# Compact sketch of q and repeated 1/den by SBUF transfers, numerators read from PSUM, and a new order of all work

## The chip, the cores and the metric

The kernel runs on one core of one Trainium2 chip. The metric is device time in microseconds (us); the time of a kernel is the median of its runs. Five engines work side by side and meet through semaphores: TensorE (PE, matmuls; PEld is its weight load), VectorE (DVE), ScalarE (ACT), GpSimd (POOL), and SyncE (SP), which here only issues DMA transfers.

## The reference

Two stages follow each other: linear attention with a sketched polynomial feature map, and an RWKV channel mix. Batch 4, 4 heads, 1088 positions, head size 32, sketch size r = 8, model width 128, inner width 1024, all float32.

```python
def phi(x):
    a = np.einsum('rd,bhsd->bhsr', S1, x)
    b = np.einsum('rd,bhsd->bhsr', S2, x)
    return np.einsum('bhsi,bhsj->bhsij', a, b).reshape(*x.shape[:-1], r * r)
q_p, k_p = (phi(q), phi(k))
kv = np.einsum('bhsf,bhsd->bhfd', k_p, v)
z = np.sum(k_p, axis=2)
num = np.einsum('bhsf,bhfd->bhsd', q_p, kv)
den = np.einsum('bhsf,bhf->bhs', q_p, z)[..., None] + 1e-06
x = num / den            # heads side by side: (4, 1088, 128)
...
xk = mu_k * x + (1.0 - mu_k) * x_prev      # x_prev: x one position earlier
xr = mu_r * x + (1.0 - mu_r) * x_prev
k = np.maximum(xk @ w_k, 0.0)
out = sigmoid(xr @ w_r) * (k * k @ w_v)
```

## The kernel before

All work is written as a list of numbered operations. Each has an engine (for some, one of several), a function that issues its instructions, and the tiles that it uses. The string ORDER names all of them once, in the order in which they are issued; since each engine takes its instructions in order, ORDER fixes the order on every engine and on SP's transfer queue. "85.1" means operation 85 by its second way (another engine), "26*5" means five filler matmuls in front. BANKS gives each PSUM tile one of the eight banks, in the order in which they were asked for.

A batch passes through three stages. Positions are cut into 34 blocks of 32.

- stage_k: DVE transposes k in 32 x 32 blocks (kT), PE makes both sketches of k (ab), DVE transposes them back (abT) and multiplies all pairs (phk, three parts). PE sums phk with v, and with ones for z, into kv. DVE masks this into w, and SP copies w with its halves exchanged (ws).
- stage_q, in two parts of 9 and 8 blocks (EX) and two halves z: DVE transposes q (qT). PE makes the sketches (ex): for x = 0 the sketch a, each row already repeated 8 times, for x = 1 the sketch b, repeated the other way. ACT copies a out of PSUM (a_sb, 8 copies for a batch), DVE multiplies it by b (phq, 8 of them). PE makes the numerators (num, 2 steps), and ACT copies them to SBUF (4 copies). PE makes the denominators (den); DVE transposes them (dT), adds 1e-6, takes the reciprocal and transposes again (rT). PE spreads 1/den over the partitions of each head, with a selection matrix sel (pr, four PSUM banks). DVE multiplies numerators and pr into x (four x for a batch, tile xT) and wraps the last block around for the shift by one position (wrap).
- stage_m, in chunks of 12, 12 and 10 blocks (CH): uk = (1 - mu_k) x on ACT or DVE; xk on DVE; xb, x in bfloat16, on GpSimd. For each chunk: 8 up-projections on PE (up), ReLU on ACT or DVE (kr), the square on DVE or ACT (k2), 3 down-projections of 8 matmuls (rd), the gate (rg), its sigmoid on ACT (sg), the product on DVE (o), and four stores. In names such as xk1.2, 1 is the batch and 2 the chunk.

Stages of different batches overlap: the sketches of batch 1 are made while batch 0 passes through stage_q. Loads go by SP's queue, a few of the first by ACT's. The filler matmuls (stir) multiply a zero tile.

Lines of the profile: kT L296, ab L303, abT L310, phk L317, kv L326, w L336, ws L337, qT L350, ex L362, a_sb L374, phq L379, num L393 and its copy L400, den L410, dT L420, the reciprocal L424 to L426, pr L436, x L445, wrap L450 and L451, uk L465 (ACT) or L467 (DVE), xk L469, xb L476, up L490, kr L495 or L497, k2 L499 or L501, rg L516, rd L521, sg L528, o L530, stores L534, stir L544.

Of the kernel before, what the change touches and what calls it, by code (L numbers as in the profile page):

```python
# [11 lines left out]
F32 = mybir.dt.float32  # L12
# [9 lines left out]
class _Buf:  # L22


    def __init__(self, pool, tag, bufs, shape, dtype):
        self.pool, self.tag, self.bufs, self.shape, self.dtype = pool, tag, bufs, shape, dtype
        self.t = None

# [4 lines left out]
class _Plan:  # L33
# [7 lines left out]
    def op(self, eng, cost, name, fn, need=(), uses=(), mode=None, kb=None, after=0.0, alt=(), stir=None):  # L41
        need = [n for n in need if n is not None]
        after = max([after] + [n["at"] for n in need if "at" in n])
        o = {"ways": [(eng, cost, fn)] + list(alt), "name": name, "need": [n for n in need if "at" not in n],
             "uses": list(uses), "mode": mode, "kb": kb, "after": after, "n": len(self.ops), "stir": stir}
        self.ops.append(o)
        return o
# [18 lines left out]
def kernel(  # L66
# [14 lines left out]
    nc = tc.nc  # L81
# [14 lines left out]
    HT = NB // 2  # L96
    EX = [(0, NT), (NT, HT - NT)]
# [3 lines left out]
        "0 9 11 10 14 12 15 13 25 18 26*5 2 34 32 28 36 37*4 43 41 16 178 190 20 17 158 45 159 27 30 39 "  # L101
        "33 29 35 31 19 21 22 179 38 44 191 197 42 169 195 40 167 193 46 180*4 4 199 188 332 192 321 1 "
        "160 344 184 200 196 194 186 163 198 164 3 182 23 161 162 24 53 54 345*2 171 353 165 5 55 6 351 "
        "333 50*1 347 349 47 52 181 185 51 189 48 49 183 168 56 166 59 170 58 172 57 62 173 312 187 65 7 "
        "334 338 342 174 63 83 323 336 86 340 60 84 175 73 314 74 176 87 313 335 343 66 339 78 81 79 341 "
        "76 77 82 85.1 317 61 68 315 88 102 71 89 72 318 103 316 75.1 337 70.2 319 112 177 207 208 204 "
        "206 320 201 110 113 325 111 209 322 324 205 326 327 69 203 210 213 202 80.1 212 486 105 328 214 "
        "90.1 466 106 67.2 114.1 146 147 329 64.2 107 468 108 144 211 134 135 100 101 467 145 120 141 142 "
        "346 487 354 352 348 124 216 350 469 470 104.1 219 471 472 330 331 355 356 498 488 496 494 361 "
        "217 115 109 362 363 492 490 215 357 476 475 136 116 137 224.2 473 149 153 358 221.2 474 360 359 "  # L110
        "129 130 117 118 91 8 232 233 364 366 479 95 131 132 119.1 368 477 478 367 499 501 503 218.2 365 "
        "481 480 505 489 495 491 373 507 220 139 140 497 143.1 369 148.1 482 500 504 94 259 506 266 376 "
        "483 484 92 138.1 508 121 493 227 228 225 226 264 265 93 267.1 502 377 260 485 254 255 122 96 230 "
        "231 375.2 123 256 271 133 269 370.1 245 125 127 272.1 99 257 258 222 261 249 274 229 278 268 234 "
        "512 514.1 270 273 509 262 515 372.2 516 240 510 511 447 371 513 242 263.1 128 151 237 243 223 "
        "517 235 241 448 150 449 236 439 450 244 454 455 238.1 152 451 300 440 288 289 378.2 301 276 97 "
        "295 296 154 155 374 452 277 290 156 453 456 291 518 298 520 157 437 275 239.1 438 521 299 283 "
        "457 284 522 444 461 279 519 293 98 396 523 441 247 397 280 524.1 294 297 292 285 303 286 445 442 "
        "246 302 394 420 443 446 425 526.2 530.1 248 395 426 287 126 250 253 251 421 391 531 389 532.2 "
        "390 386 392 398 307 418 460 423 424 459 419 458 462 465 387 384 427 603 422 381 382 304 385 604 "  # L120
        "428 379 380.1 553 252 281 608 432 557 609 611 606 305 607 393 591 592 596 601 602 615 306 525 "
        "545 383 598 599 388 401 308 605 527.1 543 597 600 593 544 415 533 416 282 309 310 528 400 594 "
        "610 595 546 399 535 408 409 534.1 403 463 402 536 404 464 410 413 414.1 579 580 529.2 613 411 "
        "412 548 549 547.1 538 311 614 612 405 550 551 562 417 616 540 541 574 406 539.1 429 577 552 575 "
        "567 618 578 537 568 569 617 430 542 563 407 619 431 433 434 570 436 572 564 565 571 566 556 554 "
        "573 555 576 582 435 581.1 558 560 559 584 585 561 586 583 587 588 589 590"
    )
    BANKS = (
        "054372056015416746272436032403465462631307721250511136240634316143716530157052706521532432014274"
        "263007616560411752054524720471305026165757704246716507671601271147100120305274343510263470306126"  # L130
        "73473657504533632672152467274272461077351"
    )
    KP = 1
# [13 lines left out]
    def ps(shape=(P, 512)):  # L147

        pair = shape[1:] == [KP, 512] and KP == 2
        t = _Buf(psum, None, 1, list(shape), F32)  # L150
        t.kind = "pair" if pair else "bank"
        banks.append(t)
        return t

    def dve(n, rate=0.96e3):
        return n / rate + 0.067

    def act(n, ptr=False):
        return n / 1.2e3 + (0.195 if ptr else 0.05)
# [12 lines left out]
    kin = [const.tile([P, NB, D], F32, name=f"kin{b}") for b in range(3)]  # L172
    qin = [const.tile([P, NB, D], F32, name=f"qin{b}") for b in range(3)]
    vts = [const.tile([P, H + 1, NT, D], F32, name=f"vt{b}") for b in range(3)]
    qTs = [const.tile([P, NB, 32], F32, name=f"qT{i}") for i in range(2)]
    LKB = NB * D * P * 4 / 1024

    def load_k(b, cuts, queues=(nc.sync,)):
        src = k[b].rearrange("h (sp t) d -> (h sp) t d", sp=32)
        for lo, hi, queue in zip(cuts, cuts[1:], queues):  # L180
            queue.dma_start(kin[b % 3][:, lo:hi, :], src[:, lo:hi, :])
# [39 lines left out]
    sel = const.tile([P, H, D], F32)  # L221
    nc.gpsimd.memset(sel[:], 0.0)
    for g in range(4):
        nc.gpsimd.affine_select(out=sel[:], in_=sel[:], compare_op=ALU.not_equal, fill=1.0, base=-32 * g,
                                pattern=[[-R, H], [0, D]], channel_multiplier=1)
# [3 lines left out]
    rz = [const.tile([P, NT, H, R], F32, name=f"rz{i}") for i in range(2)]  # L229
    for i in range(2):  # L230
        nc.gpsimd.memset(rz[i][:], 0.0)
# [6 lines left out]
                         _ap(mask4[:], [mask4[:].ap[0], [0, 2], [R, H], [1, R]]))  # L238
    WS = const.tile([P, 2, R * R], F32)
# [3 lines left out]
    def ws():  # L243
        nc.vector.tensor_copy(WS[:, 0].rearrange("p (j i) -> p j i", j=R), _ap(St[:, 0, :], [sp_, [0, R], [1, R]]))
        nc.vector.tensor_copy(WS[:, 1].rearrange("p (j i) -> p j i", j=R), _ap(St[:, 1, :], [sp_, [1, R], [0, R]]))

    o_ws = op("DVE", 0.25, "ws", ws, after=3.4)


    def sync(tile_, src, after, kb):  # L250
        return op("SP", 0.55, "in", lambda: nc.sync.dma_start(tile_, src), after=after, kb=kb)

    IN = {("k", 0): {"at": 3.7}, ("v", 0): {"at": 6.0}, ("q", 0): {"at": 7.2}}
    done = {}

    def arrival(nm, b):
        if (nm, b) not in IN:
            t = ARRIVE[nm][b]
            need = done[nm, b - 3] if b > 2 else []
            if nm == "k":  # L260
                IN[nm, b] = op("SP", 0.55, f"k{b}", lambda: load_k(b, [0, NB]), need, kb=LKB, after=t)
            elif nm == "q":
                IN[nm, b] = op("SP", 0.55, f"q{b}", lambda: load_q(b), need, kb=LKB, after=t)
            else:
                IN[nm, b] = [op("SP", 0.6, f"v{b}", lambda g=g: load_v(b, g, nc.sync), need, kb=LKB / 4, after=t)
                             for g in range(4)]
        return IN[nm, b] if isinstance(IN[nm, b], list) else [IN[nm, b]]

    ARRIVE = {"k": [0, 4, 12, 30], "v": [0, 4, 12, 30], "q": [0, 4, 12, 30]}
    i_mu = [sync(mu[:, 0:1], moe_mu_k.rearrange("d -> d ()"), 4.0, 1),  # L270
            sync(mu[:, 1:2], moe_mu_r.rearrange("d -> d ()"), 4.0, 1),
            sync(wr_f[:], moe_w_r, 4.0, 64)]
    i_wk = sync(wk_f[:], moe_w_k, 4.0, 512)
    i_wv = sync(wv_f[:], moe_w_v.rearrange("(c p) d -> p c d", p=P), 4.0, 512)
# [6 lines left out]
    o_mu = op("POOL", 1.9, "mu", prep, i_mu)  # L281
    o_wk = op("POOL", 1.1, "wk", lambda: nc.gpsimd.tensor_copy(wk[:], wk_f[:]), [i_wk])
    o_wv = op("POOL", 1.1, "wv", lambda: nc.gpsimd.tensor_copy(wv[:], wv_f[:]), [i_wv])

    QT = {B: []}
    XR = [None] * B

    def stage_k(b):
        kT = sb("kT", [P, NB, 32])
# [6 lines left out]
        tr = [op("DVE", dve(544) + 0.02, f"kT{b}", lambda lo=lo, hi=hi: nc.vector.transpose(  # L296
# [286 lines left out]
```

## Time and profile before

| | |
|---|---|
| median of 3 runs | 97.46 us (97.28 to 97.94) |
| profiled execution, its own time | 98.09 us |
| span in the profile | 96.0 us |
| busy: PE, PEld | 85.3 us, 53.3 us |
| busy: DVE, ACT, POOL | 82.7 us, 68.0 us, 17.1 us |
| mean granted TensorE clock | 0.984 |
| DMA: moved in all | 10.53 MB |

The span is the profiler's view of one execution; times of runs include what lies around it. Busy time is the time in which an engine has an instruction in work. On PE instructions overlap and their ends are modelled, so a busy PE is not PE at its peak. In timelines and in the chain of waits the first column is the start within the span and the second the duration, both in us; "x4" is the number of instructions that a line sums up, and what stands in brackets is the idle time of the engine in front of the first, with what ended it.

### The profile page before, as it was taken

How to read it: one execution, taken by the hardware profiler on the slowest of the kernel's cores; microseconds unless marked ns; L12 is line 12 of the kernel's file. 1: busy time of each engine (PE TensorE's matmuls, PEld its weight loads, DVE VectorE, ACT ScalarE, POOL GpSimd, SP SyncE). 2: the span in 40 equal slices, each digit the busy share in tenths (PEclk: the TensorE clock that was granted, in tenths of full speed). 3: DMA queues.
4: the chain of work that ended last, by engine and by line, in shares of the span. 5: the costliest groups of instructions: out<-in, count | busy, mean ns of one | idle time of the engine just before them, and what ended most of it. 6: DMA issues, size and time to landing. Idle time of an engine off the chain costs nothing.

```text
span 96.0 us, 3286 instructions
## 1 busy us (share of the span) xinstructions
PE 85.3 (89%) x1316; PEld 53.3 (55%) x1316; DVE 82.7 (86%) x187; ACT 68.0 (71%) x172; POOL 17.1 (18%) x45
## 2 busy tenths in 40 slices
PE   5949999799999999899998999999997999999800
PEld 1313474343575457553465579567584787789700
DVE  1268979979999999999979999999999999999510
ACT  0600540552719999998998799999999799999400
POOL 6850000180000050000087520000027000000000
PEclk9999999999999999999999999999999999999985
DMA  0999999299200396006200001220230133424442
GB/s 5 253 344 266 363 262 314 58 259 295 68 10 0 85 310 230 0 21 175 71 0 7 0 7 27 62 55 0 62 82 0 27 85 83 108 53 105 89 103 48
DMA packets 11279, 10.53 MB, mean 110 GB/s; under 512 B 1920, under 2 KB 9984, under 8 KB 11264
## 3 DMA queue, kind: packets, MB, share of 16 engines
q1 hardware_dynamic: 10608, 9.38, 36.2%
q10 hardware_dynamic: 656, 0.95, 3.3%
q8 instruction: 10, 0.16, 0.7%
q14 instruction: 5, 0.04, 0.2%
HBM read 7.83 MB, written 2.23 MB: 105 GB/s over the span
## 4 chain that ended last, share of the span: by engine, by line
PE 36%; DVE 31%; DMA 13%; ACT 10%; issue 4%; SPq 1%; DVEq 0%; ACTq 0%
DMA kin<-in_k_dram 13%; PE bank L521 12%; PE bank L490 9%; DVE phk L317 8%; ACT kr L495 7%; DVE phq L379 5%; DVE k L499 4%; DVE xT L445 4%; PE bank L362 3%; PE bank L516 3%; PE bank L303 3%; DVE xk L469 2%; PE bank L410 2%; ACT a_sb L374 2%; DVE o L530 2%
## 5 line engine op out<-in xcount | busy, mean ns | idle before, releaser
L495 ACT ACTIVATE kr<-bank 128x384 bf16<-128x384 f32 (+1 forms) x89 | 35.9, 531 | 1.7 <-PE bank L490 1.3
L490 PE MATMUL bank<-xk,wk 128*128 128x384 bf16 (+1 forms) x96 | 22.9, 318 | 0.4 <-DVE w L336 0.3
L521 PE MATMUL bank<-wv,k 128*128 128x128 bf16 x288 | 20.8, 219 | 0.6 <-DVE k L499 0.6
L374 ACT COPY a_sb<-bank 128x288 f32<-128x288 f32 (+1 forms) x32 | 10.1, 397 | 14.8 <-PE bank L362 14.8
L521 PEld LDWEIGHTS <-k 128*128 128x128 bf16 x288 | 18.2, 98 | 4.2 <-DVE k L499 1.1
L499 DVE TENSOR_TENSOR k<-kr 128x768 bf16<-128x768 bf16 (+1 forms) x34 | 17.7, 552 | 0.1
L476 POOL CAST xb<-xT 128x416 bf16<-128x416 f32 (+2 forms) x12 | 8.8, 758 | 42.8 <-DVE xT L451 27.1
L362 PE MATMUL bank<-qT,WS 32*64 32x288 f32 (+1 forms) x256 | 12.6, 411 | 0.2 <-DVE w L336 0.2
L379 DVE TENSOR_TENSOR phq<-bank,a_sb 128x288 f32<-128x288 f32 (+1 forms) x32 | 12.1, 422 | 0.6 <-PE bank L362 0.5
L317 DVE TENSOR_TENSOR phk<-abT 128x768 f32<-128x768 f32 x12 | 12.3, 1033 | 0.0
L490 PEld LDWEIGHTS <-wk 128*128 128x128 bf16 x96 | 7.9, 97 | 6.8 <-issue 5.0
L501 ACT ACTIVATE k<-kr 128x768 bf16<-128x768 bf16 (+1 forms) x14 | 11.5, 844 | 0.1
L326 PEld LDWEIGHTS bank<-vt,phk 128*64 128x64 f32 x288 | 9.1, 138 | 3.5 <-DVE phk L317 1.8
L326 PE MATMUL bank<-vt,phk 128*64 128x64 f32 x288 | 10.4, 225 | 0.6 <-DVE phk L317 0.5
L544 PE MATMUL bank<-idle 128*128 128x512 bf16 x28 | 8.5, 442 | 1.8 <-DVE idle L167 1.2
L362 PEld LDWEIGHTS bank<-qT,WS 32*64 32x64 f32 x256 | 4.8, 130 | 5.0 <-issue 1.7
L530 DVE TENSOR_TENSOR o<-bank,sg 128x384 f32<-128x384 f32 x12 | 6.6, 549 | 1.1 <-PE bank L521 1.1
L296 DVE STREAM_TRANSPOSE kT<-kin 128x544 f32<-128x544 f32 x8 | 5.8, 731 | 1.8 <-DMA kin<-in_k_dram 1.7
L469 DVE SCALAR_TENSOR_TENSOR xk<-xT,mu,uk 128x384 bf16<-128x384 f32 (+1 forms) x12 | 6.9, 578 | 0.0
L445 DVE TENSOR_TENSOR xT<-num,bank 128x256 f32<-128x256 f32 (+1 forms) x16 | 6.2, 426 | 0.5 <-PE bank L436 0.5
L544 PEld LDWEIGHTS <-idle 128*128 128x128 bf16 x28 | 2.6, 109 | 7.1 <-issue 3.2
L465 ACT ACTIVATE uk<-xT,omu 128x384 f32<-128x384 f32 (+1 forms) x8 | 4.7, 596 | 2.7 <-DVE xT L445 2.7
(56 smaller groups left out, 94.9 us busy)
## 6 DMA issues: line engine op xcount, KB each, us to landing
out_dram<-o SPq DMA_DIRECT2D x42, 48.0 KB, 1.6
vt<-in_v_dram SPq DMA_DIRECT2D x12, 144.0 KB, 5.3
qin<-in_q_dram SPq DMA_DIRECT2D x3, 544.0 KB, 6.5
kin<-in_k_dram SPq DMA_DIRECT2D x3, 544.0 KB, 6.8
qin<-in_q_dram ACTq DMA_DIRECT2D x1, 544.0 KB, 6.0
wk_f<-in_moe_w_k_dram SPq DMA_DIRECT2D x1, 512.0 KB, 6.9
wv_f<-in_moe_w_v_dram SPq DMA_DIRECT2D x1, 512.0 KB, 4.8
vt<-in_v_dram SPq DMA_DIRECT2D x4, 112.0 KB, 6.2
```

What stands on the lines that cost most here:

```text
L317: nc.vector.tensor_mul(phk[:, lo:hi].rearrange("p t h j i -> p (t h) j i"), a_bc, b_bc)
L326: nc.tensor.matmul(kv[64 * u:64 * u + 64, p, :], phk[:, t, h, :, :].rearrange("p j i -> p (j i)"), _ap(vt[:, h, t, :], [pv, [(H - h) * NT ...
L362: nc.tensor.matmul(px[x][p][z][64 * v_:64 * v_ + 64, :n * 32], WS[32 * h:32 * h + 32, x, :], fl(qT[32 * h:32 * h + 32], t, t + n), start=T ...
L374: copy(a_sb[:, :n * 32], pa[:, :n * 32])
L379: lambda p=p, t=t, pb=px[1][p][z], a_sb=a_sb, n=n: nc.vector.tensor_mul(fl(phq[:, p], t, t + n), pb[:, :n * 32], a_sb[:, :n * 32]),
L445: xo[g] = op("DVE", dve(n * 32), f"x{b}", lambda g=g, t=t, n=n, lo=lo: nc.vector.tensor_mul(fl(xT, 1 + t, 1 + t + n), fl(num, t, t + n), p ...
L490: nc.tensor.matmul(kp[:, i, :n * 32], wk[:, (c + i) * P:(c + i + 1) * P], fl(xk, c0, c0 + n), start=True, stop=True)
L495: o2.append(op("ACT", act(n * 32 * KP), f"kr{b}.{ci}", lambda kp=kp, kr=kr, i0=i0, n=n: nc.scalar.activation(kr[:, i0:i0 + KP, :n * 32], k ...
L499: ok.append(op("DVE", dve(n * 64, 1.92e3), f"k2{b}.{ci}", lambda k2=k2, kr=kr, cc=cc, n=n: nc.vector.tensor_mul(k2[:, 2 * cc:2 * cc + 2, : ...
L501: alt=[("ACT", act(n * 64) + 0.1, lambda k2=k2, kr=kr, cc=cc, n=n: nc.scalar.activation(k2[:, 2 * cc:2 * cc + 2, :n * 32], kr[:, :, :n * 3 ...
L521: nc.tensor.matmul(rd[:, i, :], k2[:, c, first[i]:first[i] + P], wv[:, c, :], start=(c == 0), stop=(c == NFF - 1))
L544: nc.tensor.matmul(t[:, :], idle[:, :P], idle[:], start=True, stop=True, skip_group_check=True)
```

## The change

The kernel's arithmetic stays; the work is cut up and placed differently.

- The sketch a of q: for batches 1 to 3 (FAR = 1) PE makes it without the repetition, 16 rows for each quarter of the positions, in 8 matmuls (ac). Two copies bring it to SBUF, and four SBUF transfers on SP's queue (as), each from 16 partitions, write it 8 times over to a_sb. Batch 0 keeps the old way.
- 1/den: the reciprocal is transposed with each value repeated for 8 columns, and four SBUF transfers on SP's queue (rs) write it four times over, to the partitions of each head (tile r). The matrix sel, the matmuls pr and the zeroed tiles rz go.
- Numerators are not copied: num is issued after den, and x reads the numerators from PSUM and 1/den from r.
- uk has GpSimd as a third way; wrap has GpSimd and ACT as ways, and the zero column of xT is written once at the start, in two fixed tiles. xb has ACT as second way. Each of the four stores of a chunk is an operation of its own and may go by SP's queue or ACT's.
- kin has two buffers instead of three, kT and uk one instead of two. In phk and in the sketches the two pair indices are exchanged.
- ORDER and BANKS are new. Read out by kind, operations whose engine or number differs (a filler matmul is counted by itself):

| | before | after |
|---|---|---|
| a copies | 32 ACT | 14 ACT |
| numerator copies | 15 ACT, 1 DVE | none |
| squares k2 | 34 DVE, 14 ACT | 26 DVE, 22 ACT |
| uk | 8 ACT, 4 DVE | 1 ACT, 11 POOL |
| xb | 12 POOL | 11 POOL, 1 ACT |
| wrap | 4 DVE | 4 POOL |
| ex (16 traced matmuls each) | 16 | 10 |
| ac, pr | none, 4 | 3, none |
| as, rs transfers | none | 12, 16 |
| stores' queue | 46 SP, 2 ACT | 42 SP, 6 ACT |
| filler matmuls | 28 | 19 |

Around the first x of batch 0 the order on DVE was "dT0 phk1 x2, rT0 qT2 phq1 x3, x0 x3, phk1 phq1 xk0.1 x0", with four phq1 ahead of it; it becomes "dT0 abT1 rT0 qT2 phk1 x2, x0 x2, phk1 xk0.1 x0 x2, kT2 x2, phq1 ...", with no phq1 ahead of it.

```diff
+    maskA = const.tile([P, 2, 2, 2, R], F32)
+    nc.gpsimd.memset(maskA[:], 0.0)
+    for z in range(2):
+        for h in range(H):
+            nc.gpsimd.memset(maskA[32 * h:32 * h + 32, z, :, h % 2 ^ z, :], 1.0)
...
+    SkA = const.tile([P, 2, 32], F32)
+    nc.vector.tensor_mul(SkA[:].rearrange("p z (w r) -> p (z w) r", r=R), _ap(St[:, 0, :], [sp_, [0, 8], [1, R]]),
+                         maskA[:].rearrange("p z w v r -> p (z w v) r"))
...
+        if b >= FAR:
+            pa = [ps() for _ in range(2)]
+            ac = sb("ac", [P, 2, NT * 32])
+
+            def compact():
+                for g in range(4):
+                    for p in range(2):
+                        nc.tensor.matmul(pa[p][32 * g:32 * g + 32, :NT * 32], SkA[64 * p:64 * p + 64, g // 2, :],
+                                         fl(qT[64 * p:64 * p + 64], TD[g], TD[g] + NT), start=True, stop=True)
...
+            def spread_a(g):
+                src = _ap(ac[32 * g:32 * g + 16], [[ac[:].ap[0][0], 16], [0, R], [1, 2 * NT * 32]])
+                nc.sync.dma_start(a_sb[:, g].rearrange("w p t -> w (p t)"), src)
...
+        def recip():
+            nc.vector.tensor_scalar(rc[:], dT[:].rearrange("p t h r -> p (t h) r")[:, :, 0], 1e-6, None, op0=ALU.add)
+            nc.vector.reciprocal(rr[:], rc[:])
+            nc.vector.transpose(rT[:].rearrange("p t (h r) -> p (t h) r", r=R), _ap(rr[:], [rr[:].ap[0], [1, NT * H], [0, R]]))
...
+        def spread_r(g):
+            lo = LO[g]
+            src = _ap(rT[32 * g:32 * g + 32, lo], [[rT[:].ap[0][0], 32], [0, 4], [1, (NT - lo) * 32]])
+            nc.sync.dma_start(fl(r, TD[g] + lo, TD[g] + NT), src)
...
-                o_num.append(op("ACT", act(n * 32), f"nc{b}", lambda keep=keep: keep(nc.scalar.copy), [on], [pn[z], num],
-                                alt=[("DVE", dve(n * 32), lambda keep=keep: keep(nc.vector.tensor_copy))]))
...
-                nc.tensor.matmul(pr[g][:, :NT * 32], sel[gs].rearrange("p h d -> p (h d)"),
-                                 rT[gs, :, :].rearrange("p t s -> p (t s)"), start=True, stop=True)
...
+                xo[g] = op("DVE", n * 32, f"x{b}", lambda pn=pn, t=t, n=n, z=z: nc.vector.tensor_mul(
+                    fl(xT, 1 + t, 1 + t + n), pn[z][:, :n * 32], fl(r, t, t + n)), [on, o_r[g]], [pn[z], r, xT])
...
+                     ("POOL", n * 32, lambda c0=c0, n=n: nc.gpsimd.tensor_scalar(
                     fl(uk, c0, c0 + n), fl(xT, c0, c0 + n), omu[:, 0:1], None, op0=ALU.mult))])
```

## The prediction

> **What bounds the kernel now.** I read the summary of busy time, then the busy time by stretches of the span, then the chain of waits, then single instructions in the timeline. The stretches say most (columns: stretch and its length, then the busy time of each engine with its instruction count, the granted TensorE clock, the DMA share and GB/s):
>
> ```profile
> 14.00:20.00 6.00, 5.09 (x102) 2.46 (x102) 5.48 (x14) 1.79 (x7) 1.16 (x3) 1.00 0.63 186
> 20.00:30.00 10.00, 9.96 (x195) 5.46 (x190) 9.80 (x23) 4.80 (x16) 1.18 (x2) 1.00 0.50 143
> ...
> 50.00:60.00 10.00, 9.46 (x186) 7.16 (x181) 9.96 (x24) 8.88 (x21) 4.23 (x5) 1.00 0.05 10
> 60.00:70.00 10.00, 9.82 (x138) 6.38 (x136) 9.86 (x25) 9.95 (x26) 0.00 (x0) 1.00 0.22 48
> ...
> 80.00:90.00 10.00, 10.00 (x142) 8.58 (x140) 9.86 (x23) 9.71 (x26) 0.00 (x0) 1.00 0.39 86
> ```
>
> The third busy column, VectorE (DVE), has hardly a gap from 20 us on; PE and ACT are nearly as full from 30 us on. But a busy PE overstates its work. Where PE runs freely in the chain, eight down-projection matmuls take 0.45 us, an up-projection 0.14 to 0.16, six gate matmuls 0.34: 36, 96 and 12 of these are 35 us. The float32 steps still to come at 30 us (6 kv of 0.8, 6 ex of 0.67, 6 num of 0.5, 3 den of 1.0, 4 ab of 0.57, 3 pr of 0.7) are 19: together 54 us of 61. So I take DVE as the bound from 20 to 91 us. The chain of waits shows how batch 0 reaches the first up-projection (start, duration, what):
>
> ```profile
> 17.59 1.04 PE bank L544 x4
> ...
> 22.20 0.48 DVE dT L420
> 22.68 1.71 DVE phk L317 x2
> ...
> 25.01 0.48 DVE rT L426
> ...
> 26.07 0.96 DVE phq L379 x3
> 27.03 0.11 issue
> 27.14 1.11 DVE xT L445 x3
> ```
>
> Work of batch 1 (phk, phq) stands on DVE ahead of and between the steps of batch 0, and four filler matmuls stand on PE. The first xk follows at 29.39, the first up-projection at 30.05 us.
>
> **Removed from DVE after the first xk.** By the two orders, DVE keeps 26 of 34 squares (k2): three took 1.49 us (384 columns) or 1.28 (320), so 8 x 0.48 = 3.8 us. The 4 uk on DVE go to GpSimd (59.28 to 59.60 us start to start): 1.3. One numerator copy: 0.3. Four wraps, 0.09 on the path each (the zeroing is done once at the start): 0.4. Together 5.8 us. Moved to behind the first xk: the 8 phq of batch 1, 0.36 each (four in 1.38 to 1.51 us), 2.9, and one more x of batch 0, 0.4. Net for this part: -2.5 us.
>
> **Ahead of the first xk.** The same 8 phq and one x leave this part: -3.3 us. Four of the phq and two phk (3.4 us) no longer stand ahead of rT of batch 0, so rT should end near 25.5 - 3.4 = 22.1 us.
>
> **1/den by transfers.** PE's four selection matmuls per batch (3.3 us in all) go; instead SP issues four transfers of 144 KB (two 128) behind rT, which x waits for. No such SBUF transfer is in the trace. The nearest rows are v loads of the same size, in the stretches 14 to 25 and 25 to 36 us, and a 32 KB SBUF transfer, ws, in the latter (KB each, median us from issue to landing):
>
> ```profile
> vt<-in_v_dram SPq DMA_DIRECT2D x2, 144.0 KB, 5.3
> ...
> vt<-in_v_dram SPq DMA_DIRECT2D x2, 144.0 KB, 2.7
> ws<-w SPq DMA_DIRECT2D x2, 32.0 KB, 1.8
> ```
>
> So 1.8 to 5.3 us; I take 2.7, as most of the loads are over by then, plus 0.5 us for an issue (four v loads took 2.01 us of SP): the first x can run 3.2 us after rT. Cover on DVE between rT and the first x, by the new order: batch 0 a qT and two phk, 0.71 + 1.84 = 2.55; batch 1 o, phk, two qT, three phq, w, 3.9; batch 2 two phk, xk, o, 2.65; batch 3 five k2, kr, two o, 3.9. Waits: 0.65 in batch 0, 0.55 in batch 2, none in 1 and 3: +1.2 us. Behind a waiting x on DVE stand the next batch's transposes and phq, so a wait there is paid in full. Behind rs on SP stand the as transfers, v loads, and stores.
>
> **The a sketch.** For batches 1 to 3 eight narrow matmuls, two copies and four SBUF transfers of 288 KB replace 16 matmuls and 8 copies per batch. ACT loses 18 copies of a and 15 of numerators (0.32 each where four stand in a row, 10.6 us) and 7 uk (0.59, 4.1), and takes 8 squares (0.82, 6.6) and one xb (0.4): 7.7 us freed. PE loses six ex steps (0.67 each, 4.0) and the 3.3, and takes three compact sketches: 16 traced matmuls each, as in an ex, 2.0 if alike. Neither sets the end by this trace, so I count nothing. The transfers: by the 144 KB row once to twice its 2.7 us, I take 4.1. The first is issued behind the four rs at 24.6 us and lands at 28.7; phq of batch 1 is due about 29.7: hidden, with 1 us to spare; batches 2 and 3 are issued far ahead.
>
> In the Trainium skill, "SBUF — State Buffer", section "Door 1: The DMA port swizzle", 16 partitions reach only 4 of 16 DMA ports, about 104 GB/s; by that I estimate 2.8 us of moving per transfer from its 16 source partitions, and twice that for two that share ports, and phq of batch 1 would wait about 2 us. No run shows it yet.
>
> **GpSimd.** It takes 11 of 12 uk and the wraps, so wrap, uk and xb of a batch then run there in a row. Its price is not in the trace. The nearest row is the same operation with a per-partition scalar, and the casts (start, duration):
>
> ```profile
> 19.01 0.61 POOL L278 TENSOR_SCALAR wr<-wr_f,mu 128x128 bf16<-128x128 f32 x1
> ...
> 33.53 1.38 POOL L476 CAST xb<-xT 128x416 bf16<-128x416 f32 x3 [12.35 <-DVE xT L451]
> ...
> 71.31 2.41 POOL L476 CAST xb<-xT 128x384 bf16<-128x384 f32 x3 [15.23 <-DVE uk L467]
> ```
>
> Low end 0.46 us each (three casts in 1.38); high end 1.45 (0.19 for omu's 2 columns, 0.61 for 128, drawn on to 384). I take 1.0, between a cast and the wr line. In the new order DVE has 1.3 to 2.3 us of other work between the last x needed and the first xk of batches 1 to 3, so this is covered; at 1.45, batch 3 would wait 0.3.
>
> It also slows DVE. The squares beside those last three casts:
>
> ```profile
> 71.28 2.85 DVE L499 TENSOR_TENSOR k<-kr 128x768 bf16<-128x768 bf16 x4
> ...
> 86.23 1.49 DVE L499 TENSOR_TENSOR k<-kr 128x768 bf16<-128x768 bf16 x3
> ```
>
> Four take 2.85 us where 2.0 would do: 0.85 lost in 2.41 us of GpSimd, 0.36 per us. Three phk beside casts lost 0.31, 0.75 and 0.25, so the old order loses about 2.1 us. The new one has 11 x 1.0 + 11 x 0.5 = 16.5 us of GpSimd; squares, phk and xk, which read two SBUF operands, are 32 of 75 us of DVE, so 16.5 x 0.43 x 0.36 = 2.6 us, with ends 1.6 and 3.2. Net +0.5 us (-0.5 to +1.1).
>
> The rule behind it, in the Trainium skill, "SBUF — State Buffer", section "Who interferes with whom", speaks against the change: a DVE instruction with two SBUF inputs and a GpSimd one that reads SBUF exclude each other, and the second blocks fully. By that all of 16.5 x 0.43 = 7.1 us would be lost; the trace agrees that they collide, but shows 0.36 of it.
>
> Nine of 28 filler matmuls go; the clock was 1.00 in every stretch to 90 us, so I count nothing. The setup on GpSimd (11 memsets, near 0.1 us each, in place of 2.1 us for sel and rz) and one more DVE product of 0.23 us lie ahead of the k load's landing, for which DVE waits 1.06 us now. The tail from the last o (91.5) to 96.0 us stays: its last stores go out by two queues before and after.
>
> **Sum.** -2.5 - 3.3 + 1.2 + 0.5 = -4.1 us: the span 96.0 becomes 91.9. The profiled execution took 98.09 us, 2.1 more than its span and 0.6 above the median 97.46; from the median, 93.4 us.
>
> **Rivals.**
> - *More gain (91.1 us).* The order puts waits nowhere and a uk costs as a cast: no 1.2, and -0.5 instead of +0.5: -6.3 us. For it: ACT, full in 30 to 40 and 60 to 70 us, is 7.7 us lighter, which could also close small gaps.
> - *GpSimd excludes DVE wholly (97.9).* 7.1 instead of 2.6 us is +4.5 on the forecast. Against it: the 0.36 measured. For it: uk is longer than a cast, so more work collides. Ends by the price of uk, 95.4 and 99.7.
> - *1/den lands late: slower.* Place: x of each batch on DVE. Batches 0 and 2 lose one for one beyond 2.7 us of landing, 1 and 3 beyond 3.4. Extra 2 x (L - 2.7) + 2 x (L - 3.4) reaches the gain of 4.1 at L = 4.1 us; at the loaded row's 5.3 it is 9.0 and the time 102.4. For it: the as transfers (288 KB each) share the queue. Against: the DMA share is 0.05 to 0.25 from 40 to 80 us.
> - *No change (97).* The early part's 3.3 us is lost again waiting for the as transfers of batch 1.
> - That the change does not do what it says has no place: the steps are written out in the order.
>
> **Numbers.** Forecast 0.55 (its own range 92 to 95.5), more gain 0.23, exclusion 0.09, late 1/den 0.09, no change 0.04. Predicted 93.4. With 2 in 10 left out (the late case, most of the exclusion, the far end of the gain) the range is 90.0 to 97.0. One per cent is 0.97 us, about what a measurement here can tell from no change: faster takes the first two and a third of the exclusion, 0.81; same 0.07 (no change, a third of the exclusion); slower 0.12.
>
> **What would show it.** Right: DVE busy near 76 us; first xk near 27 us; idle before x under 1 us per batch; k2 and phk longer by a few tenths beside GpSimd. Wrong: DVE idle before x or phq ended by the transfers; uk over 1.5 us; k2 at twice 0.5; TensorE clock under 1.00 after 14 us; PE full while DVE has gaps, which would make PE the bound and my DVE sum void.

## The result, and the profile after

The changed kernel takes 112.53 us (median of 4 runs, 112.30 to 113.24) beside 97.70 us for the kernel before on the same chip (4 runs, 97.28 to 98.01): a ratio of 1.153, with a 95% interval of 1.146 to 1.161. The prediction said 93.4 us, with a range up to 97.0: wrong in sign. The profiled execution took 112.72 us, its span is 110.9 us.

The page's first part and its DMA issues (KB each, median us from issue to landing):

```profile
PE 87.0 (78%) x1227; PEld 53.0 (48%) x1227; DVE 77.8 (70%) x167; ACT 62.4 (56%) x141; POOL 27.6 (25%) x63
...
a_sb<-ac SPq DMA_DIRECT2D x12, 288.0 KB, 6.1
vt<-in_v_dram SPq DMA_DIRECT2D x12, 144.0 KB, 5.2
...
r<-rT SPq DMA_DIRECT2D x8, 144.0 KB, 4.6
r<-rT SPq DMA_DIRECT2D x8, 128.0 KB, 3.6
```

DVE is busy for 77.8 us where it was 82.7, and ACT for 62.4 where it was 68.0: the work did leave both engines. But DVE is now idle for 33 us of its span, 13 before. The busy times by stretches say where (columns as in the prediction: PE, PEld, DVE, ACT, GpSimd, granted clock, DMA share, GB/s):

```profile
14.00:20.00 6.00, 5.83 (x86) 2.12 (x77) 6.00 (x16) 1.31 (x4) 1.38 (x3) 1.00 0.57 151
...
30.00:40.00 10.00, 6.69 (x71) 3.08 (x72) 5.39 (x14) 5.77 (x14) 1.97 (x2) 0.97 0.80 170
...
50.00:60.00 10.00, 5.98 (x92) 2.59 (x77) 5.83 (x15) 5.27 (x12) 5.23 (x7) 1.00 0.64 108
60.00:70.00 10.00, 7.71 (x105) 4.15 (x105) 6.65 (x13) 5.92 (x15) 0.00 (x0) 0.83 0.85 146
...
90.00:100.00 10.00, 10.00 (x115) 8.21 (x114) 9.72 (x21) 8.85 (x22) 5.85 (x7) 0.83 0.32 65
```

From 14 to 20 us and from 90 to 100 us DVE is full, as it was. In the three stretches shown between them DVE is idle for a third to nearly half of the time, PE and ACT are not full either, and the DMA share is 0.64 to 0.85 where it was 0.05 and 0.22 from 50 to 70 us. The DMA engines are busy but do not move much: 108 and 146 GB/s, while the kernel before reached 143 GB/s at a share of 0.50. What DVE and PE wait for (us in total, times, longest):

```profile
DVE xT L454 <- DMA r<-rT: 9.4, 4, 5.1
...
DVE phq L400 <- DMA a_sb<-ac: 7.5, 3, 3.1
...
DVE qT L344 <- DMA qin<-in_q_dram: 2.4, 1, 2.4
...
PE bank L321 <- DMA vt<-in_v_dram: 2.1, 2, 1.4
```

DVE, which the prediction took as the bound, waits 19.3 us for transfers: 9.4 for 1/den, 7.5 for the sketches a, 2.4 for a load of q that stands behind them. In the chain of waits (start, duration) the transfers are among the longest links; the only other one of this length behind 20 us is a load of k (7.09 us, from 43.54):

```profile
25.22 6.71 DMA a_sb<-ac
...
51.27 7.52 DMA a_sb<-ac
...
66.03 6.81 DMA r<-rT
...
84.42 4.52 DMA r<-rT
```

The early part went as foreseen. Batch 0 on DVE (start, duration):

```profile
20.88 0.48 DVE L426 STREAM_TRANSPOSE rT<-rr 128x288 f32<-128x288 f32 x1
...
24.87 0.79 DVE L454 TENSOR_TENSOR xT<-bank,r 128x288 f32<-128x288 f32 x2 [0.90 <-DMA r<-rT]
25.57 0.95 DVE L312 TENSOR_TENSOR phk<-abT 128x768 f32<-128x768 f32 x1
26.44 0.61 DVE L477 SCALAR_TENSOR_TENSOR xk<-xT,mu,uk 128x384 bf16<-128x384 f32 x1
```

The first xk starts at 26.44 us, 2.95 us earlier than before. What was won there, and 15 us more, is lost after it.

### The profile page after: what moved, and what is told of

Its sections match the earlier page's. It is cut to its first block, busy times and chain, and to the rows that moved or that the text cites. A ratio compares the mean times of both kernels' runs of the same rounds, so it can differ in the third digit from the quotient of the medians.

```text
span 110.9 us, 3105 instructions
## 1 busy us (share of the span) xinstructions
PE 87.0 (78%) x1227; PEld 53.0 (48%) x1227; DVE 77.8 (70%) x167; ACT 62.4 (56%) x141; POOL 27.6 (25%) x63
## 2 busy tenths in 40 slices
DMA packets 15310, 16.29 MB, mean 147 GB/s; under 512 B 2368, under 2 KB 12480, under 8 KB 15296
## 3 DMA queue, kind: packets, MB, share of 16 engines
HBM read 7.83 MB, written 2.23 MB: 91 GB/s over the span
## 4 chain that ended last, share of the span: by engine, by line
DMA 35%; DVE 23%; PE 19%; SPq 12%; POOL 5%; issue 3%; DVEq 0%; POOLq 0%
DMA a_sb<-ac 13%; DMA kin<-in_k_dram 11%; DMA r<-rT 10%; PE bank L525 6%; PE bank L496 6%; DVE phq L400 4%; SPq L371 4%; DVE phk L312 3%; POOL uk L475 3%; DVE qT L344 3%; SPq L433 2%; PE bank L520 2%; SPq L181 2%; PE bank L409 2%; SPq L332 2%
## 5 line engine op out<-in xcount | busy, mean ns | idle before, releaser
L499 ACT ACTIVATE kr<-bank 128x384 bf16<-128x384 f32 (+1 forms) x89 | 37.3, 494 | 19.3 <-PE bank L496 18.7
L475 POOL TENSOR_SCALAR uk<-xT,omu 128x384 f32<-128x384 f32 (+1 forms) x11 | 14.1, 1284 | 15.7 <-DVE xT L454 15.6
L400 DVE TENSOR_TENSOR phq<-bank,a_sb 128x256 f32<-128x256 f32 (+1 forms) x32 | 12.3, 427 | 8.0 <-DMA a_sb<-ac 7.5
L505 ACT ACTIVATE k<-kr 128x768 bf16<-128x768 bf16 (+1 forms) x22 | 17.7, 828 | 0.0
L503 DVE TENSOR_TENSOR k<-kr 128x768 bf16<-128x768 bf16 (+1 forms) x26 | 13.1, 541 | 0.0
L454 DVE TENSOR_TENSOR xT<-bank,r 128x288 f32<-128x288 f32 (+1 forms) x16 | 6.2, 433 | 9.4 <-DMA r<-rT 9.4
L382 PE MATMUL bank<-qT,WS 32*64 32x256 f32 (+1 forms) x160 | 9.3, 410 | 1.3 <-DVE qT L344 0.8
L298 PE MATMUL bank<-kT,Skb 128*32 128x288 f32 x64 | 5.7, 415 | 3.1 <-DVE phq L400 2.5
L531 ACT ACTIVATE sg<-bank 128x384 f32<-128x384 f32 x12 | 6.1, 535 | 2.2 <-PE bank L520 2.1
L344 DVE STREAM_TRANSPOSE qT<-qin 128x512 f32<-128x512 f32 (+1 forms) x8 | 5.7, 716 | 2.4 <-DMA qin<-in_q_dram 2.4
L481 POOL CAST xb<-xT 128x320 bf16<-128x320 f32 (+2 forms) x11 | 5.8, 538 | 6.0 <-DVE xT L454 6.0
```

The lines of the kernel that those rows point to most:

```text
L344: nc.vector.transpose(qT[:].rearrange("p (z t) s -> p z (t s)", z=2)[:, :, 32 * c0:32 * (c0 + n)], qin[b % 3][:].rearrange("p (z t) d -> p ...
L382: nc.tensor.matmul(px[p][z][64 * v_:64 * v_ + 64, :n * 32], WS[32 * h:32 * h + 32, x, :], fl(qT[32 * h:32 * h + 32], t, t + n), start=True ...
L400: lambda p=p, t=t, g=g, lo=lo, pb=px[1][p][z], n=n: nc.vector.tensor_mul(fl(phq[:, p], t, t + n), pb[:, :n * 32], a_sb[:, g, p, lo:lo + n ...
L475: ("POOL", n * 32, lambda c0=c0, n=n: nc.gpsimd.tensor_scalar(fl(uk, c0, c0 + n), fl(xT, c0, c0 + n), omu[:, 0:1], None, op0=ALU.mult))])
L499: o2.append(op("ACT", n * 32, f"kr{b}.{ci}", lambda kp=kp, kr=kr, i=i, n=n: nc.scalar.activation(kr[:, i, :n * 32], kp[:, :n * 32], ACTF.R ...
L503: ok.append(op("DVE", n * 64, f"k2{b}.{ci}", lambda k2=k2, kr=kr, cc=cc, n=n: nc.vector.tensor_mul(k2[:, 2 * cc:2 * cc + 2, :n * 32], kr[: ...
```

## The experiments

Theory after the result: the DMA engines are the new bound between 20 and 90 us. The twelve transfers of a read 16 partitions each, move slowly, and whatever stands behind them is late. Rivals: the transfers of 1/den are to blame; SP's line of issues is, not the engines behind it; the new order itself is bad, whatever the transfers do.

**1 to 3: each set of transfers left out, then both.** The tile that they would write is replaced by a constant one; the matmuls and copies that make their sources stay. So no_as multiplies by a constant in place of a in batches 1 to 3, no_rs by 1 in place of 1/den, no_both does both.

```diff
-                nc.sync.dma_start(a_sb[:, g].rearrange("w p t -> w (p t)"), src)    # no_as, no_both
+                pass
...
-            nc.sync.dma_start(fl(r, TD[g] + lo, TD[g] + NT), src)                   # no_rs, no_both
+            pass
```

> The 12 a transfers of batches 1 to 3 are left out; phq of these batches multiplies by a constant tile instead. Theory 1 (the SBUF transfers fill the DMA engines and SP's queue, and DVE waits for them and for the loads behind them): the a transfers are 3.5 of the 5.8 MB added and stand in front of rs, v and q loads, so without them rs lands in about 3 us, v in about 3, and the time is 95 to 99 us. Theory 2 (the new order with GpSimd in it is slow by itself, and the waits only show where it is late): less than 5 us of the 15 are won, 108 us or more.

> The 16 transfers of 1/den are left out; x multiplies by a constant tile instead. Theory 1: the 9.4 us that x waits for them go, but the a transfers still hold up phq and the loads: 102 to 106 us. Theory 2: 108 us or more.

> Both kinds of transfers are left out, with constant tiles in their place; all instructions on PE, DVE, ACT and GpSimd stay, in the same order. Theory 1: what is left is the sum of the prediction without its 1.2 us of waits, 91 to 94 us, GpSimd included. Theory 2: still over 105 us. Between the two, 95 to 105, both have a part.

One run each, beside 97.86 us for the kernel before on that chip: no_as 96.62, no_rs 102.75, no_both 91.02. All three fall inside what theory 1 gave. From 91.0, the 1/den transfers alone cost 5.6 us, those of a alone 11.7, both 21.5 (with 112.53); the other 4.2 us appear only when both are there. Without transfers the engines are full again; no_both by stretches:

```profile
30.00:40.00 10.00, 10.00 (x184) 6.25 (x177) 9.93 (x22) 9.69 (x23) 1.05 (x1) 1.00 0.54 168
...
60.00:70.00 10.00, 9.94 (x143) 7.12 (x141) 9.45 (x24) 9.83 (x25) 2.93 (x6) 1.00 0.17 34
```

So the order is not to blame: with its transfers free it is 6.8 us faster than the kernel before. But 1/den is not harmless either; no_as still waits for it, at a landing of 3.3 us (144 KB):

```profile
DVE xT L456 <- DMA r<-rT: 4.9, 6, 1.3
```

**4: the transfers alone (micro).** A kernel that computes nothing of the reference: one transfer, then four in a row, from 16, 32 or 128 partitions, each followed by a DVE copy that reads the tile written.

```diff
+        for g in range(4):
+            nc.sync.dma_start(d[g][:], _ap(t[32 * g:32 * g + 16], [[t[:].ap[0][0], 16], [0, 8], [1, N]]))
...
+            nc.sync.dma_start(d[g][:], _ap(t[32 * g:32 * g + 32], [[t[:].ap[0][0], 32], [0, 4], [1, N]]))
...
+            nc.sync.dma_start(d[g][:], _ap(t[:], [[t[:].ap[0][0], P], [1, N]]))
```

> Only transfers, each kind alone or four at once, one kind after the other; nothing of the reference is computed and the output is zeros. Theory 1a (the few source partitions are what is slow): four transfers of 288 KB from 16 partitions each take over 1.5 times the four from 128 partitions, and one alone also. Theory 1b (any SBUF transfer of this size costs that much, whatever its source): the two differ by less than 15%, and both take longer than four loads of 288 KB from HBM. For 1/den, 32 partitions against 128, the same question at 144 KB.

Issues on SP (start, duration of four issues) for 288 KB from 16, 32 and 128 partitions:

```profile
14.32 6.35 SPq L60 DMA_DIRECT2D a_four<-s  x4
27.48 4.63 SPq L64 DMA_DIRECT2D a_four<-s  x4
35.69 2.47 SPq L68 DMA_DIRECT2D a_four<-s  x4
```

and the copies on DVE that start when each has landed, the four from 16 partitions and then the last from 32 and from 128:

```profile
19.36 0.15 DVE L41 COPY s<-a_four 128x1 f32<-128x1 f32 x1 [5.06 <-DMA a_four<-s]
21.90 0.15 DVE L41 COPY s<-a_four 128x1 f32<-128x1 f32 x1 [2.39 <-DMA a_four<-s]
24.85 0.15 DVE L41 COPY s<-a_four 128x1 f32<-128x1 f32 x1 [2.80 <-DMA a_four<-s]
27.30 0.15 DVE L41 COPY s<-a_four 128x1 f32<-128x1 f32 x1 [2.29 <-DMA a_four<-s]
...
35.51 0.15 DVE L41 COPY s<-a_four 128x1 f32<-128x1 f32 x1 [1.09 <-DMA a_four<-s]
...
40.36 0.15 DVE L41 COPY s<-a_four 128x1 f32<-128x1 f32 x1 [0.59 <-DMA a_four<-s]
```

From 16 partitions, four take 13.0 us (14.32 to 27.30) and land about 2.6 us apart, one behind the other although their sources lie in four different places. From 32 they take 8.0 us and land 1.28 apart, from 128 4.7 us and 0.72 apart. By these distances the same 288 KB move at 113, 230 and 410 GB/s. The rule that the prediction cited, in the Trainium skill's "SBUF — State Buffer", section "Door 1: The DMA port swizzle", lets the rate depend on the ports that a transfer's partitions reach. The trace agrees, with the partitions of the source: the prediction's estimate by that rule, 2.8 us of moving per transfer, stands beside 2.6 measured. Four transfers as 1/den needs them (144 KB from 32 partitions) take 4.8 us, and a single one lands after 2.7 (9.17 to 11.84).

**5: the a transfers issued by ACT (as_act).** This takes them out of SP's line and leaves their bytes and their sources.

```diff
-                nc.sync.dma_start(a_sb[:, g].rearrange("w p t -> w (p t)"), src)
+                nc.scalar.dma_start(a_sb[:, g].rearrange("w p t -> w (p t)"), src)
```

> The 12 a transfers are issued by ACT instead of SP, at the same places of the order, so SP's own issues and those behind them no longer stand in line with them. If what costs the time is the line at SP, rs, v and ws are issued on time and land in 3 to 4 us: 100 to 105 us. If it is that the DMA engines themselves are taken by slow reads from 16 partitions, rs and v land as late as before, however they are issued, and ACT stands still during its own issues: 109 us or more.

Measured 114.27 us (before: 97.88): no gain, DVE still waits 9.2 us for 1/den and 7.0 for a. SP's own issues stay slow although no a transfer stands in its line any more; the four of 1/den in batch 2 took 6.20 us in the change (from 66.03) and take 8.16 us here (from 63.62). So the a transfers hold up the others without standing in their line; what both queues share is the limit, not SP's line by itself. (ACT pays for its own issues here, up to 2.86 us for one.) The Trainium skill's "DMA: Bandwidth & Descriptors", section "Issuing engines are not separate DMA queues", says that a second issuing engine brings no second set of DMA engines; this run agrees.

**6: the same bytes from 32 partitions (as32).** In the change PE already writes each row of the compact sketch twice (32 rows for each quarter of the positions), and a transfer reads 16 of them. Here the two copies are laid out as neighbours, so that a transfer reads 32 partitions and repeats four times instead of eight.

```diff
-    maskA = const.tile([P, 2, 2, 2, R], F32)
+    maskA = const.tile([P, 2, 2, R, 2], F32)
...
-                src = _ap(ac[32 * g:32 * g + 16], [[ac[:].ap[0][0], 16], [0, R], [1, 2 * NT * 32]])
+                src = _ap(ac[32 * g:32 * g + 32], [[ac[:].ap[0][0], 32], [0, 4], [1, 2 * NT * 32]])
```

> The two copies of the compact sketch that PE makes anyway are laid out as neighbours, so that each a transfer reads 32 partitions four times over instead of 16 partitions eight times; bytes, instructions and result are the same. With transfers alone on the chip, four took 8.0 us from 32 partitions and 12.9 from 16. If the span of the source is the cause, some 5 us of DMA time less per batch take away a third to a half of the 15.9 us that the a transfers cost: 104 to 108 us. If the bytes or the number of transfers were the cause, nothing changes: over 111.

Measured 105.08 us (before: 97.88). Nothing but the source of the transfers and the setup of their columns differs (15310 DMA packets and 16.29 MB in both), and 7.4 us of the 14.8 are gone. The issue row:

```profile
a_sb<-ac SPq DMA_DIRECT2D x12, 288.0 KB, 4.5
```

**7 and 8: as32 with half the bytes (as32_bf), and with two of four 1/den transfers issued by ACT (as32_bf_ract).** Both round a to bfloat16.

```diff
-        a_sb = sb("a_sb", [P, 4, 2, NT * 32])
+        a_sb = sb("a_sb", [P, 4, 2, NT * 32], BF16)
...
-            ac = sb("ac", [P, 2, NT * 32])
+            ac = sb("ac", [P, 2, NT * 32], BF16)
...
-            nc.sync.dma_start(fl(r, TD[g] + lo, TD[g] + NT), src)                               # ract only
+            (nc.scalar if g in (2, 0) else nc.sync).dma_start(fl(r, TD[g] + lo, TD[g] + NT), src)
```

> As the one before, and the compact sketch and its repeated copy are kept in bfloat16, half the bytes (the sketch a of q is rounded to bfloat16). By the times of transfers alone, some 4 to 4.5 us per batch instead of 12.9: the a transfers then cost 2 to 4 us in place of 15.9, 98 to 101 us. If a fixed cost for each transfer or its issue were what counts, it stays over 103.

> As the one before, and two of the four 1/den transfers of each batch are issued by ACT, so that the four issues of 0.6 us each stand in two lines. If x waits for the line of issues, 1 to 3 us less than the one before; if it waits for the landing itself, the same within 0.7 us; if ACT loses more by waiting for rT than x gains, more time.

as32_bf took 96.62 us, below the 98 to 101 that were expected and as much as no_as: at 144 KB from 32 partitions the a transfers cost nothing that shows. as32_bf_ract took 100.81: x waits 7.1 us in place of 4.6. The largest part is in batch 0: ACT's second issue came at 26.13 us, 5.2 us behind the end of rT, because a uk stood ahead of it on ACT and waited there for the first x; x then waited 3.55 us for what that issue brought.

**9 to 11: the a sketch made the old way.** far4 takes the compact sketch and its transfers out for all batches and keeps 1/den by transfers and uk on GpSimd. PE makes the repeated a in four steps for a batch, ACT copies it; these operations were placed into the order by hand. far4_late moves x of two batches later and issues the 1/den transfers of batch 3 in a row; far4_late_uk also puts the 11 uk of GpSimd on ACT.

```diff
-                nc.sync.dma_start(a_sb[:, g].rearrange("w p t -> w (p t)"), src)
...
+                                nc.tensor.matmul(pa[z][64 * v_:64 * v_ + 64, :n * 32], WS[32 * h:32 * h + 32, 0, :],
+                                                 fl(qT[32 * h:32 * h + 32], t, t + n), start=True, stop=True)
...
+                            copy(a_sb[:, g, p, 32 * LO[g]:32 * LO[g] + n * 32], pz[:, :n * 32])
```

> The sketch a of batches 1 to 3 is made the old way again, in four steps of two banks each (PE writes it already repeated, ACT copies 8 tiles for a batch); the a transfers are gone, all else, 1/den by transfers and GpSimd included, stays as changed, in the new order. Against the kernel without a transfers (96.6 us) this adds some 2 us of PE and 6 us of ACT. If DVE is the bound, as the prediction had it, both are hidden: 96 to 98.5 us, and so the a transfers alone turned a gain into a loss. If PE or ACT have become the bound: 99 to 103 us.

> As the one before, with x of batches 0 and 2 placed a few DVE instructions later, and the four 1/den transfers of batch 3 issued one behind the other, ahead of a store. In the kernel without a transfers x waited 4.9 us in all for 1/den to land. If that wait is a plain loss on DVE, 1.5 to 4 us less than the one before: 93.5 to 96.5 us, faster than both kernels. If what stands behind x (uk on GpSimd, xk, up-projections) is then late by as much, the same within 0.7 us.

> As the one before, with the 11 uk of GpSimd put on ACT, at the same places. It measures what GpSimd is worth: by the prediction, a uk takes 1.0 us there and slows DVE by 0.5 us in sum, and ACT, which has room now, needs 0.6: so the same within 1 us if ACT has the time. If GpSimd's longer uk (1.08 to 1.8 us in the trace) holds up xk or its use of the SBUF ports holds up DVE, 1 us or more faster; if ACT is in the way of the kr of the up-projections, 1 us or more slower.

far4 took 103.92 us, a ratio of 1.061 (1.051 to 1.071) to 97.73 for the kernel before; far4_late 105.13, 1.077 (1.069 to 1.085); far4_late_uk 106.77 in one run. far4 ended just above its slower branch and far4_late outside both of its own; far4_late_uk fell into its third (1 us or more slower). The waits of far4:

```profile
ACT a_sb L365 <- PE bank L359: 11.6, 9, 3.8
...
DVE abT L305 <- PE bank L298: 6.4, 4, 2.9
...
PE bank L321 <- DMA vt<-in_v_dram: 3.1, 1, 3.1
...
DVE xT L447 <- DMA r<-rT: 1.8, 5, 0.6
```

Here x hardly waits (1.8 us), but ACT waits for PE's sketches and DVE for the sketches of k: in this order the engines wait on each other. Whether the placing by hand is at fault or the work that PE and ACT take back, these runs do not separate. So far4 says that one such order is slow, not what the old sketch of a would cost in a good one. far4_late fits that x was not the limit there: its x waits 1.4 us, and the time is no better. Moving uk from GpSimd to ACT adds 1.6 us (106.77 less 105.13), by one run where the runs of far4 alone lie up to 1.9 us apart; its trace points the same way, since xk waits 5.0 us for uk on ACT. So GpSimd looks like the better place for uk in that order, which is a hint and no more.

**12: 128 source partitions, the same bytes (as_wide).** Each transfer reads 128 partitions without repetition, so the tile that it writes is not the repeated sketch.

```diff
-                src = _ap(ac[32 * g:32 * g + 16], [[ac[:].ap[0][0], 16], [0, R], [1, 2 * NT * 32]])
+                src = _ap(ac[:], [[ac[:].ap[0][0], P], [1, 2 * NT * 32]])
```

> Each a transfer reads all 128 partitions of the compact tile once, in place of 16 partitions eight times: the same 288 KB in rows of the same length, the same number of transfers, in the same places; what it writes is not the repeated sketch a. Alone on the chip four such transfers took 4.7 us, against 12.9 from 16 partitions and 8.0 from 32, and four of half the bytes from 32 partitions 4.8. If the time that four transfers need is what counts, whether it comes from the bytes or from the source, this stands near the bfloat16 kernel, whose transfers cost nothing next to none at all: 96 to 99 us. If the bytes written count for themselves, it stands near the kernel with 32 source partitions: 103 to 106 us.

Measured 98.48 us beside 99.34 for the kernel before on that chip, a ratio of 0.991, or 97.0 on the scale of the other runs (97.86). Size, number, place and queue of the transfers are those of the change, and so are the 15310 DMA packets and 16.29 MB of the whole kernel; only the sources are wide. The issue row and DVE's waits:

```profile
a_sb<-ac SPq DMA_DIRECT2D x12, 288.0 KB, 3.8
```

```profile
DVE xT L454 <- DMA r<-rT: 4.6, 5, 1.2
...
DVE phq L400 <- DMA a_sb<-ac: 1.3, 2, 0.9
```

Side by side, what four transfers need when alone and what the twelve cost in the kernel, over the 96.62 us of no_as:

| a transfer | four alone | twelve in the kernel |
|---|---|---|
| 288 KB from 16 partitions | 13.0 us | +15.9 us (112.53) |
| 288 KB from 32 | 8.0 us | +8.5 us (105.08) |
| 288 KB from 128 | 4.7 us | +0.4 us (97.0) |
| 144 KB from 32 | 4.8 us | 0.0 us (96.62) |

The cost follows the time that the transfers occupy the DMA engines, not their bytes: the last two rows move different amounts in the same time and cost the same. But for the 112.53, each time here is one run, uncertain by about 1%, so the last two rows are zero within that.

## Why the prediction was wrong

**The step that failed** is in "The a sketch": "The transfers: by the 144 KB row once to twice its 2.7 us, I take 4.1", "hidden, with 1 us to spare", and with them "I count nothing". The landing was 6.1 us in the median. But the size of one landing was the smaller error: the waits of phq, the only reader that was looked at, are 7.5 us of the 15.9 that the transfers cost. I charged a transfer only if its own reader came too soon, and charged nothing to what stands behind it. Four of them take 13 us even alone, and 1/den, loads of v and q, and the next sketches all pass the same engines. SP's timeline shows such a place at 22 us (start and duration of the issues; the first four are 1/den of batch 0):

```profile
21.39 3.12 SPq L433 DMA_DIRECT2D r<-rT  x4
24.61 3.54 SPq L371 DMA_DIRECT2D a_sb<-ac  x3
28.19 2.72 SPq L186 DMA_DIRECT2D vt<-in_v_dram  x1
```

One v load there takes SP 2.72 us to issue, where four took 2.01 before. Leaving the a transfers out gives back 15.9 us (no_as), and the same bytes from 128 partitions give back 15.5 (as_wide, on the scale above).

The argument "the DMA share is 0.05 to 0.25 from 40 to 80 us" failed with it: that share was read from a trace without the 5.8 MB that the change adds (16.29 MB moved in place of 10.53). The prediction's own estimate from the Trainium skill, 2.8 us of moving per transfer, would have given 34 us of DMA time for twelve (an estimate); I used it for one reader alone, phq of batch 1, which it had wait about 2 us. That one waited 1.47 us, those of batches 2 and 3 waited 3.14 and 2.92.

**1/den by transfers** was mis-sized in the same direction: landing 2.7 us taken, which is what one takes alone, but 4.6 and 3.6 measured for the two sizes, and 3.3 and 3.2 even without the a transfers. Waits of 1.2 us were forecast, 9.4 came (0.90, 1.20, 5.11 and 2.23 in batches 0 to 3, where 0.65, 0, 0.55 and 0 stood); 4.9 in no_as. With the a transfers away, this term is what makes no_as 96.6 us instead of 91.0. The rival "1/den lands late" named the right place, x on DVE, and its point of no gain, a landing of 4.1 us, lies between the two medians; its price was too low, because the longest landing was not 5.3 but 6.8 us in the chain, and because phq and qT wait as well. DVE's timeline shows the longest wait, in batch 2:

```profile
67.28 0.55 DVE L533 TENSOR_TENSOR o<-bank,sg 128x384 f32<-128x384 f32 x1
72.94 1.16 DVE L454 TENSOR_TENSOR xT<-bank,r 128x288 f32<-128x288 f32 x3 [5.11 <-DMA r<-rT]
```

**DVE as the bound, and the sum on it,** fit what is left without the transfers. Without the two waits the prediction's sum is -5.3 us, 92.2; the rival "more gain" said 91.1; no_both took 91.02, 6.8 us less than the kernel before beside it. What the single terms are worth was not measured one by one, and PE and ACT are as full as DVE in no_both, so that DVE is the bound there is not shown.

**Ahead of the first xk:** rT ended at 21.36 us (forecast near 22.1), the first xk started 2.95 us earlier (forecast 3.3), with a wait of 0.90 us (forecast 0.65). Held.

**GpSimd:** a uk took 1.28 us in the mean, above the 1.0 taken and inside its bounds; xk took 0.68 us in place of 0.58, k2 0.54 in place of 0.55 and phk 0.95 in place of 1.03, so the few tenths more that were expected in those two do not show in their means. The groups (busy, mean ns of one, idle before):

```profile
L475 POOL TENSOR_SCALAR uk<-xT,omu 128x384 f32<-128x384 f32 (+1 forms) x11 | 14.1, 1284 | 15.7 <-DVE xT L454 15.6
...
L477 DVE SCALAR_TENSOR_TENSOR xk<-xT,mu,uk 128x384 bf16<-128x384 f32 (+1 forms) x12 | 8.1, 682 | 0.6 <-POOL uk L475 0.6
```

The slowdown in xk is 12 x 0.10 = 1.2 us. The rival of complete exclusion put 7.1 us on DVE; without the waits it would stand at 96.7 us (97.9 less 1.2), and no_both, with all of the GpSimd work, took 91.02. So that price fell, but not exclusion itself. The prediction read the collision on DVE alone: beside the four squares that lost 0.85 us, its lines show three casts in 2.41 us where three took 1.38 elsewhere, so GpSimd lost about as much. The rule behind that rival, in the Trainium skill's "SBUF — State Buffer", section "Who interferes with whom", has whichever engine comes second wait for the other, so the loss need not fall on DVE; no run here isolates one pair.

**Fillers and clock,** counted at nothing, were not quite nothing. The clock falls after some of the waits. PE idles 1.97 us up to 89.54, ended by x, which had waited for 1/den:

```profile
89.54 0.63 PE L496 MATMUL bank<-xk,wk 128*128 128x320 bf16 x3 [1.97 <-DVE xT L454]
```

Then the clock falls (stretch, busy times, granted clock):

```profile
91.00:92.00 1.00, 1.00 (x6) 0.50 (x5) 0.82 (x2) 0.61 (x2) 1.00 (x2) 0.50 0.45 90
92.00:93.00 1.00, 1.00 (x11) 0.89 (x9) 1.00 (x3) 0.95 (x3) 1.00 (x3) 0.50 0.00 0
93.00:94.00 1.00, 1.00 (x9) 0.72 (x7) 1.00 (x3) 1.00 (x3) 1.00 (x1) 0.50 0.38 76
```

PE is full at half its clock for these 3 us. The same happens twice before, after idle times of 2.82 us (up to 38.46) and 2.52 us (up to 59.29), both ended by phq, which had waited for a: the granted clock is 0.50 from 40 to 42 us and from 60 to 63 us. After an idle time of 2.29 us (up to 67.43) it stayed at 1.00. In no_both, with no such waits and the same fillers, the clock is 1.00 throughout, which fits that this follows from the waits. DVE's waits for transfers, 19.3 us, leave 2.2 of the 21.5 us between no_both and the change; the halved clock may be part of that rest but was not tested by itself.

**Open:** whether the new order with the old sketch of a, well placed, would beat the kernel before. No version with the full computation did; the fastest, far4, took 103.92 us.

## What to carry to other kernels

When work is moved from an engine to transfers, the transfers' time on the DMA engines, at the rate of their source's partitions, is a term of the sum like any engine's: add it up over all of them, and charge every reader of the queue that stands behind. A DMA share read from the trace before does not yet tell the room that is left once the change has added its own transfers. If data must be repeated over partitions, let the source lie in as many partitions as the matmul that makes it can fill: 32 in place of 16 gave back half of the loss here, though not yet a gain. And replacing a transfer's target by a constant tile shows within one run what that transfer costs, where that is well above the noise.

## What the runs showed of the hardware

- Four transfers from 16 partitions each, in four different quarters of the 128 partitions, did not run side by side in micro: they landed about 2.6 us apart, as one behind another.
- An issue on SP took 0.50 us in micro with no other transfer under way (288 KB from 128 partitions), and up to 2.72 us in the change (the v load above) with slow transfers ahead of it. Why the issue itself grows is open.
- Idle times of PE of 2.82, 2.52 and 1.97 us were each followed by about 3.4 us at a granted clock of 0.50, from 0.6 to 1.1 us after PE had resumed (worked out from stretches of 1 us); one of 2.29 us was not. So the length of the idle time alone did not decide it.
